# One-column products widened to 128 equal columns, and the odd outputs' row as a full-height product

## The chip, the cores and the metric

The kernel runs on one core of a Trainium2 chip. The metric is device time in microseconds (us) of one execution. The engines are TensorE (PE in the profile, with its weight loads as PEld), VectorE (DVE), ScalarE (ACT), GpSimd (POOL) and SyncE (SP, which here issues DMAs). A float32 matmul is recorded as two MATMUL and two LDWEIGHTS records, so record counts are twice the counts in the code; a float32r matmul is one of each.

## The reference

Attention with decay, an FFT mixer with an FFN behind it, and a gated convolution, on 2 x 768 tokens of 512 features:

```python
x = attention(q, k, v, lam)                       # (2, 768, 512), float32
X = np.fft.fft(np.fft.fft(x, axis=1), axis=2)
u = x + np.real(X)
var = np.mean((u - np.mean(u, -1, keepdims=True)) ** 2, axis=-1, keepdims=True)
un = (u - mean) / np.sqrt(var + 1e-06)
x = u + np.maximum(un @ w_ch1, 0.0) @ w_ch2
out = (sigmoid(causal_conv5(x, conv_w)) * (x @ w_val)) @ w_out
```

The change touches the real part of the FFT and the variance.

## The kernel before

The attention goes by chunks of 128 tokens (6 a batch, `att_*`), the FFT by batch (`fft_*`), the layer norm, FFN and gate by blocks of 384 tokens (k = 0 to 3, two a batch). Features lie on the partitions, in four tiles. There is no loop over the work: `ORDER` is a list of tokens, written out, one for each step (`XD0,1,0` is `fft_D` of batch 0, j 1, w 0; `G0,3,2` is `ffn2`), and each engine runs its part of the list in that order. A plus sign puts an elementwise step on VectorE and not on GpSimd. Weights come as float64 words; the steps `Dl`, `Dx`, `Da`, `Db`, `Dc`, `De` load and convert them to float32 on ACT and DVE between the other work, up to about 200 us. The FFT of batch 0 lies within the attention of batch 1, and the FFT of batch 1 within the FFN of block 0.

The FFT's real part uses symmetry. `fft_pm` (L326) forms sum (w=0) and difference (w=1) of feature pairs, `fft_fold` (L337) adds or subtracts token s and S-s into `F`. `fft_D` (L373) multiplies tiles of `F` (as weights) with the table `cd`: 257 cosine columns for w=0, 256 sine columns for w=1. `fft_P` and `fft_Q` (L399, L389) multiply its result `AB` with the token tables; `fft_P256` (L424) does so for the one column 256. Feature row 0 is special: its even outputs want the sum and its odd outputs the difference. The table has zeros in row 0 at odd columns, and `fft_fx` (L342) forms the row for the odd outputs; `fft_fxh` and `fft_fxl` (L346, L349) split it in two float32r halves, and two one-row matmuls (L376) add it to all odd columns, with a row `oddr` of zeros and ones as the moving operand. In `F` for w=1, row 0 of the first tile meets only sin 0 = 0. `fft_a384` (L357, L359) makes the terms of token 384: eight matmuls whose moving operand is one column, two of them with one row (`odd`), two with one-column weights. `ln_var` (L567) sums squares over the features by a matmul with one column of `ones`, for each 128 tokens: 12 matmuls for block 0 (four tiles each), 3 for each later block. `ln_newton` takes the inverse root on DVE, `ln_diag` (L593, ACT) spreads it on a diagonal and `ln_spread` (L600, TensorE) over the partitions. `pe_fill` (L198) is eight records of `ident` with `ones`, all columns equal, at 8 us. The PSUM pool `ps_o` has two banks; all of these steps take turns in it.

Of the kernel before, what the change touches and what calls it, by code (L numbers as in the profile page):

```python
# [7 lines left out]
F32 = mybir.dt.float32  # L8
F32R = mybir.dt.float32r
AF = mybir.ActivationFunctionType  # L10
# [6 lines left out]
P = 128  # L17
# [26 lines left out]
    "L": "load_chunk", "Z": "pe_fill", "K": "lam_powers", "S": "att_S", "s": "att_pm", "k": "att_kd_act", "A": "att_AV", "E": "att_inter", "T": "att_ST", "t": "att_st", "X": "x_shift",  # L44
    "Xcd": "fft_cd", "Xcs": "fft_cs", "XD": "fft_D", "XA": "fft_a384", "XQ": "fft_Q", "XP": "fft_P", "Xc": "fft_pc",
# [8 lines left out]
    "Kq": "att_qs", "Y": "att_decay", "Xm": "fft_pm", "Xe": "fft_edge", "Xo": "fft_fold", "Xx": "fft_fx", "Xl": "fft_fxl", "Xp": "fft_mp", "Xu": "u_add",  # L54
# [5 lines left out]
Xcs1 S0,0,0 S0,0,1 Z4 L0,1 s0,0,0 s0,0,1 K A0,0 k0,0,0 k0,0,1 L0,2 T0,0 Kq0,1+ e0,0+ k0,1,0 S0,1,0 S0,1,1 t0,0 k0,1,1 T0,1 Y0,1 s0,1,0 L0,3 s0,1,1 A0,1 a0,0 Kq0,2+ t0,1 k0,2,0 S0,2,0  # L60
# [862 lines left out]
```

## Time and profile before

| what | value |
|---|---|
| three runs, us | 455.9, 457.12, 459.17 (median 457.12) |
| the profiled execution's own time, us | 459.33 |
| its span from first to last instruction, us | 457.5 |
| TensorE busy | 447.6 us, 98% |
| VectorE, ScalarE, GpSimd busy | 312.7, 244.6, 129.1 us |
| mean granted TensorE clock | 0.989 |

Busy time says that an instruction was in the engine, not how much it did there; the granted clock is 1.00 at 2.4 GHz and 0.50 at 1.2 GHz. Stages are read by their time from the span's start.

### The profile page before, as it was taken

The numbers are of one execution on the slowest core, as the hardware profiler recorded it, in microseconds if no ns is written. First come the engines' busy times: TensorE is split into PE (matmuls) and PEld (weight loads), VectorE is DVE, ScalarE is ACT, GpSimd is POOL, SyncE is SP. The second block draws the span as 40 slices with busy tenths as digits, with TensorE's granted clock in tenths as the row PEclk, the third lists the DMA queues.
The fourth block names the chain that finished last, engine by engine and source line by source line (L and its number), as shares of the span: only waits on it lengthen the run. The fifth ranks groups of instructions, "written<-read, shape, count | busy, mean of one in ns | idle before, by whom it ended". The sixth has DMA issues, their size and how long they took to land.

```text
span 457.5 us, 7094 instructions
## 1 busy us (share of the span) xinstructions
PE 447.6 (98%) x2752; PEld 396.8 (87%) x2752; DVE 312.7 (68%) x498; ACT 244.6 (53%) x501; POOL 129.1 (28%) x115
## 2 busy tenths in 40 slices
PE   8999999999999999899999999999999999999996
PEld 7887757777658779899999999999999999999994
DVE  5768489887989998885866478813736794222594
ACT  4555566756757765486436357524733844242442
POOL 1132304201041112325263446322523512430230
PEclk9999899889999999999999999999999999999999
DMA  7899951547735340000000000000000010000101
GB/s 266 287 302 318 397 160 65 177 172 255 239 140 185 100 178 1 0 3 0 1 0 24 0 1 23 1 1 24 1 1 0 24 46 1 0 1 24 47 1 69
DMA packets 15861, 40.45 MB, mean 88 GB/s; under 512 B 2012, under 2 KB 4052, under 8 KB 14804
## 3 DMA queue, kind: packets, MB, share of 16 engines
q1 hardware_dynamic: 15540, 39.62, 25.0%
q8 instruction: 21, 0.34, 0.3%
q10 hardware_dynamic: 288, 0.39, 0.3%
q14 instruction: 12, 0.10, 0.1%
HBM read 35.29 MB, written 3.15 MB: 84 GB/s over the span
## 4 chain that ended last, share of the span: by engine, by line
PE 90%; DVE 4%; DMA 2%; SPq 1%; issue 1%; ACT 1%; DVEq 0%; ACTq 0%
PE acc L636 10%; PE acc L638 10%; PE acc L637 10%; PE ph L644 8%; PE ph L638 7%; PE ph L636 7%; PE ph L637 7%; PE pso L636 4%; PE pso L637 4%; PE pso L638 4%; PE pso L373 3%; PE psS L251 3%; PE pso L266 2%; PE pso L277 2%; PE pso L399 2%; PE pso L389 2%
## 5 line engine op out<-in xcount | busy, mean ns | idle before, releaser
L636 PE MATMUL acc<-g,w2s 128*128 128x384 f32 x240 | 83.5, 348 | 1.3 <-DVE tmp L680 1.3
L637 PE MATMUL acc<-g,w2s 128*128 128x384 f32 x240 | 80.5, 335 | 0.0
L638 PE MATMUL acc<-g,w2s 128*128 128x384 f32 x240 | 80.5, 335 | 0.0
L632 POOL TENSOR_TENSOR w2s<-w,w2s 128x512 fp32r<-128x512 f32 x27 | 36.9, 1366 | 145.2 <-ACT w2s L628 130.7
L628 ACT CAST w2s<-w 128x512 fp32r<-128x512 f32 x62 | 37.9, 618 | 42.7 <-PE acc L638 42.7
L665 DVE SCALAR_TENSOR_TENSOR g<-ph,g 128x384 fp32r<-128x384 f32 x60 | 32.8, 553 | 35.3 <-ACT g L660 34.8
L731 DVE SCALAR_TENSOR_TENSOR gate<-u,cw,gate 128x384 f32<-128x384 f32 (+4 forms) x64 | 48.4, 770 | 1.6 <-ACT gate L726 0.9
L636 PEld LDWEIGHTS acc<-g,w2s 128*128 128x128 f32 x240 | 45.1, 188 | 3.7 <-DVE tmp L680 1.6
L614 ACT CAST w1s<-w 128x512 fp32r<-128x512 f32 x48 | 29.6, 618 | 34.5 <-PE ph L638 34.3
L637 PEld LDWEIGHTS acc<-g,w2s 128*128 128x128 f32 x240 | 45.1, 188 | 1.3
L660 ACT ACTIVATE g<-ph 128x384 fp32r<-128x384 f32 x60 | 28.9, 488 | 30.6 <-PE acc L638 17.2
L638 PEld LDWEIGHTS acc<-g,w2s 128*128 128x128 f32 x240 | 45.1, 188 | 0.1
L644 PE MATMUL ph<-uc,w 128*128 128x384 f32 x128 | 45.1, 501 | 0.0
L636 PE MATMUL ph<-hlA,w1s 128*128 128x384 f32 x128 | 43.4, 339 | 0.6 <-DVE g L665 0.6
L638 PE MATMUL ph<-hlA,w1s 128*128 128x384 f32 x128 | 43.1, 337 | 0.2 <-DVE w1s L618 0.2
L637 PE MATMUL ph<-hlA,w1s 128*128 128x384 f32 x128 | 42.9, 335 | 0.0
L618 POOL TENSOR_TENSOR w1s<-w,w1s 128x512 fp32r<-128x512 f32 x21 | 28.2, 1347 | 50.7 <-ACT w1s L614 36.1
L632 DVE TENSOR_TENSOR w2s<-w,w2s 128x512 fp32r<-128x512 f32 x35 | 27.3, 779 | 21.9 <-ACT w2s L628 21.7
L644 PEld LDWEIGHTS ph<-uc,w 128*128 128x128 f32 x128 | 24.8, 197 | 15.0 <-issue 1.4
L618 DVE TENSOR_TENSOR w1s<-w,w1s 128x512 fp32r<-128x512 f32 x27 | 23.0, 859 | 18.6 <-ACT w1s L614 18.6
L636 PEld LDWEIGHTS ph<-hlA,w1s 128*128 128x128 f32 x128 | 24.0, 188 | 1.3 <-DVE g L665 0.9
L638 PEld LDWEIGHTS ph<-hlA,w1s 128*128 128x128 f32 x128 | 24.0, 188 | 0.8 <-DVE w1s L618 0.8
(212 smaller groups left out, 957.4 us busy)
## 6 DMA issues: line engine op xcount, KB each, us to landing
raw<-in_w_dram SPq DMA_DIRECT2D x16, 1024.0 KB, 5.0
ldqk<-in_qT_dram SPq DMA_DIRECT2D x12, 256.0 KB, 5.7
ldqk<-in_k_dram SPq DMA_DIRECT2D x12, 256.0 KB, 5.8
ldv<-in_v_dram SPq DMA_DIRECT2D x12, 256.0 KB, 5.8
ldkT<-in_kT_dram SPq DMA_DIRECT2D x11, 256.0 KB, 6.3
out_dram<-o SPq DMA_DIRECT2D x11, 256.0 KB, 2.0
raw<-in_wv_dram SPq DMA_DIRECT2D x2, 1024.0 KB, 5.0
raw<-in_wo_dram SPq DMA_DIRECT2D x2, 1024.0 KB, 4.7
```

The costliest lines, as they stand in the source:

```text
L251: nc.tensor.matmul(r["pss"][t][:, a, :], r["kT"][hp, a, :], r["qT"][hp, a, :], start=True, stop=True)
L614: self.nc.scalar.copy(w[:, 0], self.raw1(f))
L618: eng.tensor_tensor(w[:, 1], self.raw1(f), w[:, 0].bitcast(F32), op=ALU.subtract)
L628: self.nc.scalar.copy(w[:, 0], self.raw2(f))
L632: eng.tensor_tensor(w[:, 1], self.raw2(f), w[:, 0].bitcast(F32), op=ALU.subtract)
L636: nc.tensor.matmul(out, lh, rh, start=start, stop=False)
L637: nc.tensor.matmul(out, lh, rl, start=False, stop=False)
L638: nc.tensor.matmul(out, ll, rh, start=False, stop=stop)
L644: self.nc.tensor.matmul(ph, self.raw1(f)[:, t], self.uc[k][:, t], start=(t == 0), stop=(t == 3))
L660: self.nc.scalar.activation(g[:, 0], self.ph[(k, f)], AF.Relu)
L665: self.nc.vector.scalar_tensor_tensor(g[:, 1], self.ph[(k, f)], 0.0, g[:, 0].bitcast(F32), op0=ALU.max, op1=ALU.subtract)
L731: self.nc.vector.scalar_tensor_tensor(gp[:, o:TB], x, w, gp[:, o:TB], op0=ALU.mult, op1=ALU.add)
```

## The change

Every product with one moving column now streams 128 columns, all equal. In `fft_a384` the column is repeated by a step of 0, the column groups lie 128 apart in PSUM, the one-row `odd` becomes a tile of 128 rows whose rows 1 to 127 are zero, and the group of one column takes 128 weight columns (of which one output is read). In `ln_var` the whole tile `ones` is the moving operand. `fft_P256` takes 128 weight columns. The row for the odd outputs is written into the spare row 0 of `F` (w=1), and in `fft_D` one float32 matmul of full height adds it to the 128 odd columns (output step 2, moving operand one column of `odd` repeated). `fft_fxh` and `fft_fxl` are gone; `fft_fx` comes after the last fold of its batch, ahead of `fft_D`. `AB` is one column narrower.

```diff
-        self.fx[b] = self.tmp()[0:1]
-        eng.tensor_tensor(self.fx[b], z[0:1, 1, 0, 0:HS], z[:, :, :, S:HS:-1][0:1, 1, 0, :], op=ALU.add)
-    def fft_fxh(self, b):
-        self.fxr[b] = [self.tmp(dt=F32R)[0:1] for _ in range(2)]
-        self.nc.scalar.copy(self.fxr[b][0], self.fx[b])
-    def fft_fxl(self, eng, b):
-        eng.tensor_tensor(self.fxr[b][1], self.fx[b], self.fxr[b][0].bitcast(F32), op=ALU.subtract)
+        eng.tensor_tensor(self.F[b][0:1, 1, 0, :], z[0:1, 1, 0, 0:HS], z[:, :, :, S:HS:-1][0:1, 1, 0, :], op=ALU.add)
...
     def fft_a384(self, b):
-        for g, (c0, cw) in enumerate(((0, 128), (128, 128), (256, 1))):
-            for a in range(2):
-                nc.tensor.matmul(ps[:cw, g:g + 1], cd[:, a, c0:c0 + cw], z[:, 0, a, HS:HS + 1], start=(a == 0), stop=(a == 1 and g > 1))
+        for g in range(3):
+            x = [(cd[:, a, g * P:(g + 1) * P], z[:, 0, a, HS:HS + 1]) for a in range(2)]
             if g < 2:
-                nc.tensor.matmul(ps[:, g:g + 1], self.odd[0:1, 0:128], z[0:1, 1, 0, HS:HS + 1], start=False, stop=True)
+                x.append((self.odd, z[:, 1, 0, HS:HS + 1]))
+            for n, (w, y) in enumerate(x):
+                nc.tensor.matmul(ps[:, g * P:(g + 1) * P], w, y.to_broadcast([P, P]), start=(n == 0), stop=(n == len(x) - 1))
...
     def fft_D(self, b, j, w):
         if w == 0:
-            for x in range(2):
-                nc.tensor.matmul(ps[:, 0:256], self.fxr[b][x][:, sl], self.oddr, start=False, stop=(x == 1))
+            nc.tensor.matmul(ps[:, 1:256:2], F[:, 1, 0, sl], self.odd[:, 1:2].to_broadcast([P, C]), start=False, stop=True, skip_group_check=True)
...
     def fft_P256(self, b):
-            self.nc.tensor.matmul(ps[0:1, 0:HS + 1], self.AB[b][:, j, 256:257], self.cs[0][:, j, :], start=(j == 0), stop=(j == 2))
+            self.nc.tensor.matmul(ps[:, 0:HS + 1], self.AB[b][:, j, 256:384], self.cs[0][:, j, :], start=(j == 0), stop=(j == 2))
...
     def ln_var(self, k):
-                self.nc.tensor.matmul(ps[:, t:t + 1], x[:, t * P:(t + 1) * P], self.ones[:, 0:1], start=(d == 0), stop=(d == len(qs) - 1))
+                self.nc.tensor.matmul(ps[:, t * P:(t + 1) * P], x[:, t * P:(t + 1) * P], self.ones, start=(d == 0), stop=(d == len(qs) - 1))
```

In `ORDER` the tokens move so (batch 0; batch 1 alike):

```diff
-XA0 Xo0,0,0+ Xx0+ Xo0,1,1 Dl0 T1,2 Xo0,0,1+ Xh0 S1,3,0 a1,2 Xl0 S1,3,1 Xo0,1,0+ k1,3,0 XD0,0,0
+XA0 Xo0,0,0+ Xo0,1,1 Dl0 T1,2 Xo0,0,1+ S1,3,0 a1,2 S1,3,1 Xo0,1,0+ Xx0+ k1,3,0 XD0,0,0
```

## Rows read from the trace of the kernel before

**Rows 1.** The page's part 4, the chain that ended last, by engine.

```profile
PE 90%; DVE 4%; DMA 2%; SPq 1%; issue 1%; ACT 1%; DVEq 0%; ACTq 0%
```

**Rows 2.** Span and mean granted clock of the core.

```profile
core 0: 457.5 us, clock 0.989
```

**Rows 3.** Stages: length, busy us (count) of PE, PEld, DVE, ACT, POOL; PEclk; DMA; GB/s.

```profile
41.80:42.60 0.80, 0.00 (x0) 0.00 (x0) 0.80 (x2) 0.00 (x0) 0.77 (x1) 1.00 1.06 387
42.66:44.45 1.79, 1.79 (x16) 1.73 (x16) 1.57 (x3) 0.00 (x0) 0.22 (x1) 1.00 1.10 435
...
45.10:48.40 3.30, 3.30 (x23) 2.89 (x20) 1.02 (x2) 2.39 (x10) 1.66 (x3) 0.50 1.01 395
...
80.25:82.55 2.30, 2.30 (x23) 2.30 (x22) 1.99 (x4) 2.16 (x4) 0.81 (x1) 1.00 0.72 191
82.65:85.95 3.30, 3.30 (x8) 2.09 (x8) 2.82 (x10) 2.91 (x5) 0.56 (x1) 0.50 0.93 332
...
96.35:98.05 1.70, 1.70 (x18) 1.61 (x16) 1.70 (x5) 0.20 (x1) 0.00 (x0) 1.00 1.03 422
...
99.75:103.00 3.25, 3.25 (x8) 2.21 (x7) 1.76 (x2) 1.71 (x4) 0.00 (x0) 0.50 0.29 49
...
187.50:189.70 2.20, 0.93 (x6) 0.61 (x4) 2.20 (x4) 0.62 (x1) 2.20 (x2) 1.00 0.00 0
189.80:193.00 3.20, 3.20 (x19) 3.20 (x20) 3.09 (x4) 1.00 (x2) 1.83 (x2) 1.00 0.00 0
```

**Rows 4.** The chain in order of time, 6 to 13 us: start, us, what.

```profile
6.02 2.08 PE psS L251 x16
8.10 2.00 PE pso L198 x8
...
12.01 1.14 PE psS L251 x16
```

**Rows 5.** The same chain from 40 us on, single steps of TensorE.

```profile
67.02 2.03 PE pso L424 x6
...
80.36 2.75 PE pso L567 x24
...
98.12 1.06 PE pso L373 x4
99.18 0.43 PE pso L376 x2
...
109.87 0.86 PE pso L373 x4
...
123.40 1.94 PE pso L399 x6
```

**Rows 6.** VectorE by stretch and its waits; single lines; timeline rows of ACT, PE, DVE.

```profile
70.90:104.00 33.10, 28.84 (x46) 0.90 0.47 156
104.00:168.60 64.60, 60.47 (x78) 1.00 0.55 187
...
DVE w L489 <- ACT w L485: 3.2, 3, 2.5
...
L342 DVE TENSOR_TENSOR tmp<-pm x2: 548/881/1214, 42.1 to 90.0; 1x384 f32<-1x384 f32 x2
...
L346 ACT CAST tmp<-tmp x2: 494/496/497, 44.8 to 91.4; 1x384 fp32r<-1x384 f32 x2
...
L349 POOL TENSOR_TENSOR tmp<-tmp x1: 984/984/984, 45.4 to 45.4; 1x384 fp32r<-1x384 f32 x1
L349 DVE TENSOR_TENSOR tmp<-tmp x1: 539/539/539, 93.8 to 93.8; 1x384 fp32r<-1x384 f32 x1
...
87.50 0.39 ACT L593 ACTIVATE tmp<-ident,var 128x128 fp32r<-128x128 f32 x1
...
89.42 0.81 PE L600 MATMUL pso<-tmp,onesr 128*128 128x384 f32 x2
...
95.36 1.50 DVE L337 TENSOR_TENSOR F<-pm 128x384 f32<-128x384 f32 x3
```

More of the change, by code (lines that the diff above doesn't have):

```diff
@@ L43 @@
 PLAIN = {
-    "L": "load_chunk", "Z": "pe_fill", "K": "lam_powers", "S": "att_S", "s": "att_pm", "k": "att_kd_act", "A": "att_AV", "E": "att_inter", "T": "att_ST", "t": "att_st", "X": "x_shift",
+    "L": "load_chunk", "Z": "pe_fill", "Kl": "lam_powers", "S": "att_S", "s": "att_pm", "k": "att_kd_act", "A": "att_AV", "E": "att_inter", "T": "att_ST", "t": "att_st", "X": "x_shift",
     "Xcd": "fft_cd", "Xcs": "fft_cs", "XD": "fft_D", "XA": "fft_a384", "XQ": "fft_Q", "XP": "fft_P", "Xc": "fft_pc",
[1 row of a table removed]
[1 row of a table added]
     "Np": "ln_spread",
@@ L53 @@
 GPS = {
-    "Kq": "att_qs", "Y": "att_decay", "Xm": "fft_pm", "Xe": "fft_edge", "Xo": "fft_fold", "Xx": "fft_fx", "Xl": "fft_fxl", "Xp": "fft_mp", "Xu": "u_add",
+    "Kq": "att_qs", "Y": "att_decay", "Xm": "fft_pm", "Xe": "fft_edge", "Xo": "fft_fold", "Xx": "fft_fx", "Xp": "fft_mp", "Xu": "u_add",
     "Ns": "ln_sum", "Nl": "ln_lo", "Na": "ln_acc", "u": "split1l", "v": "split2l", "R": "resid", "Ml": "m_lo", "Mk": "m_gvl",
@@ new lines @@
+F0,10 Nq1,1 v0,11+ Na1,1+ De19 F0,14 Da17 Dl20 Nl1,2+ f0,10 Db17 Nq1,2 h0,10 G0,10,0 Dc15 G0,10,3 Dx17 G0,10,1 De15 G0,10,2 G0,11,0 G0,11,2 f0,14 Dl18 Dc17 G0,11,3 V0,13 G0,11,1 h0,14
+De17 Da20 F0,13 V0,12 Dl16 Db20 Wo0 Nl1,3+ Nq1,3 u1,1+ F1,1 wo0 f0,13 h0,13 Dx18 v0,13+ Dx16 F0,15 Da16 Na1,2+ Db16 Dc16 Na1,3+ U1,0 u1,0+ Wo1 wo1+ Nv1 Dx20 v0,12+ G0,12,0 De16 Dc20
+G0,12,3 Da18 G0,12,1 G0,12,2 Db18 G0,13,3 De20 G0,13,2 f0,15 G0,13,1 V0,14 h0,15 G0,13,0 Wv0 v0,14+ F1,0 V0,15 Dc18 f1,1 Wv2 h1,1 v0,15 G0,14,1 wv2+ U1,3 G0,14,2 G0,15,1 Wv3 G0,14,0
@@ new lines @@
+Rm0,1 G0,15,0 u1,3+ G0,14,3 Rm0,0 G0,15,3 R0,1 R0,0+ F1,2 V1,0 f1,0 v1,0+ Mg0,0 h1,0 G0,15,2 Mg0,1 wv3+ F1,3 f1,2 Rm0,2 h1,2 V1,1 v1,1+ U1,6 R0,2+ Rm0,3 Ha1 G1,0,0 G1,0,3 U1,4 G1,0,1
+u1,6 Mt0,0,3 G1,0,2 G1,1,0 Mt0,0,2 G1,1,2 f1,3 u1,4 h1,3 G1,1,1 V1,2 v1,2+ G1,1,3 F1,4 V1,3 Mt0,0,1 R0,3 v1,3+ G1,2,0 G1,2,1 f1,4 h1,4 G1,2,3 U1,5 u1,5+ F1,6 Mg0,3 Mt0,0,0 Mg0,2 De18
+Ms0,0 F1,5 wv0+ U1,7 Mt0,1,3 Wo2 Mt0,1,2 Wv1 Nw1 u1,7 G1,3,3 G1,2,2 U1,10 G1,3,1 f1,6 G1,3,0 h1,6 V1,4 G1,3,2 Nd1 F1,7 v1,4+ u1,10+ wv1 Mt0,3,3 G1,4,3 f1,5 G1,4,1 U1,8 G1,4,0 V1,5
@@ new lines @@
+U3,13 h3,14 u3,10 Np3 F3,10 u3,13 F3,13 U3,15 u3,15+ G3,8,2 f3,13 Mo2,0 V3,9 h3,13 f3,10 v3,9+ h3,10 G3,9,0 G3,9,1 Me2,0 G3,9,3 G3,9,2 Mo2,1 V3,10 v3,10+ G3,10,0 G3,10,3 G3,10,1 G3,11,0
+G3,11,1 G3,11,3 G3,10,2 G3,11,2 Mo2,2 V3,13 V3,12 v3,13 v3,12+ F3,15 V3,14 V3,15 v3,14+ Me2,2 G3,12,0 v3,15+ f3,15 G3,13,0 G3,14,0 Me2,1 h3,15 G3,15,0 G3,12,1 G3,13,1 Rm3,0 G3,14,1
+R3,0+ G3,15,1 Mz3,0 G3,12,2 Mg3,0 G3,13,2 Rm3,1 Ml3,0 G3,14,2 R3,1+ G3,15,2 Mt3,0,3 Mz3,1 G3,12,3 Rm3,2 Mg3,1 G3,13,3 Ml3,1 G3,14,3 Mt3,1,3 G3,15,3 Mt3,1,2 Ev0,0 Ev1,0 R3,2+ Ev0,1
@@ L109 @@
+Mt3,0,2 Mz3,2 Ev2,0 Mt3,0,1 Mg3,2 Ev3,0 Rm3,3 Ml3,2 Ev1,1 R3,3+ Ev0,2 Ev2,1 Mt3,2,3 Mz3,3 Ev1,2 Mt3,0,0 Mg3,3 Ev2,2 Ml3,3+ Ms3,0 Ev0,3 Mt3,1,1 Ev1,3 Mt3,2,2 Ev2,3 Mx3,0 Ev3,1 Mt3,1,0
+My3,0 Ev3,2 Mt3,2,1 Ms3,1 Ev3,3 Mx3,1 Mk3,0 Eo0,0 Mt3,2,0 My3,1 Eo0,1 Mt3,3,3 Ms3,2 Eo0,2 Mk3,1 Mx3,2 Eo1,0 Mt3,3,2 My3,2 Eo1,2 Mt3,3,1 Eo1,1 Mt3,3,0 Mk3,2+ Eo2,0 Ms3,3 Eo2,2 Mx3,3
+Eo2,1 My3,3 Mk3,3+ Eo3,0 Eo3,2 Es0 Eo3,1 Es2 Es1
 """
@@ L168, in setup @@
         nc.scalar.copy(self.onesr, self.ones)
-        self.odd = self.fft.tile([1, C], F32, name="odd", tag="odd")
+        self.odd = self.fft.tile([P, C], F32, name="odd", tag="odd")
         nc.gpsimd.memset(self.odd, 0.0)
-        nc.gpsimd.memset(self.odd[:, 1:C:2], 1.0)
-        self.oddr = self.fft.tile([1, 2 * C], F32R, name="oddr", tag="oddr")
-        for x in range(2):
-            nc.scalar.copy(self.oddr[:, x * C:(x + 1) * C], self.odd)
+        nc.gpsimd.memset(self.odd[0:1, 1:C:2], 1.0)
         self.U = [p.tile([P, 4, S], F32, name=f"u{b}", tag=f"u{b}") for b in range(B)]
@@ L372, in fft_D @@
         for a in range(2):
-            nc.tensor.matmul(ps[:, 0:n], F[:, w, a, sl], cd[:, a, o:o + n], start=(a == 0), stop=(a == 1 and w == 1))
+            nc.tensor.matmul(ps[:, 0:n], F[:, w, a, sl], cd[:, a, o:o + n], start=(a == 0), stop=(a == 1), skip_group_check=True)
         if w == 0:
-            for x in range(2):
-                nc.tensor.matmul(ps[:, 0:256], self.fxr[b][x][:, sl], self.oddr, start=False, stop=(x == 1))
+            nc.tensor.matmul(ps[:, 1:256:2], F[:, 1, 0, sl], self.odd[:, 1:2].to_broadcast([P, C]), start=False, stop=True, skip_group_check=True)
     def fft_Dev(self, eng, b, j, w):
         if b not in self.AB:
-            self.AB[b] = self.fft.tile([P, 3, 514], F32, name="AB", tag="AB")
+            self.AB[b] = self.fft.tile([P, 3, 513], F32, name="AB", tag="AB")
         n = 257 if w == 0 else 256
-        o = 0 if w == 0 else 258
+        o = 0 if w == 0 else 257
         eng(self.AB[b][:, j, o:o + n], self.psD[(b, j, w)][:, 0:n])
@@ L386, in fft_Q @@
         ps = self.psQ[(b, g)] = self.ps_o.tile([P, 512], F32, name="pso2", tag="pso2")
-        o = 258 + 128 * g
+        o = 257 + 128 * g
         for j in range(3):
@@ L573, in ln_newton @@
         v, sd, r0, a = (var[:, n * j:n * j + n] for j in range(4))
[L574 removed]
+        nc.vector.tensor_scalar_add(v, self.psv[k][:, 0:TB:P], 1e-6)
         nc.scalar.activation(sd, v, AF.Sqrt)
```

85 lines of the change are left out of this document (36 added, 49 removed), and 2 rows, old and new, of the table PLAIN.

## The prediction

> **What bounds the kernel now.** I read the chain that ended last first: nine tenths of it is TensorE, so a microsecond of TensorE is a microsecond of the end, unless another engine fails to follow [rows 1]. Then the mean granted clock: 0.989 over 457.5 us is 5.1 us of full-speed time that TensorE did not get [rows 2]. Where it is lost shows in a table by stage, and the reader is to look at what TensorE did before each fall [rows 3]. It ran at 0.50 (1.2 GHz in place of 2.4) from 45.1 to 48.4, 82.65 to 85.95 and 99.75 to 103.0. Ahead of the first stands an idle stretch of 0.8 us and then, from 42.66 to 44.45, the one-column products of `fft_a384`; ahead of the second, from 80.25 on, the one-column products of `ln_var`; ahead of the third, 96.35 to 98.05, `fft_a384` of the second batch. The page calls TensorE busy in all three, but an instruction there streams one column. Each low stretch, with its edges, is 3.4 us, so it costs 1.7 us; three make 5.1 us, the whole loss. Idleness alone isn't the cause: in 187.5 to 189.7 TensorE worked 0.93 of 2.2 us, and 189.8 to 193.0 is at 1.00 [rows 3].
>
> **The clock.** The change makes these products 128 columns wide. Do 128 equal columns keep the clock where one does not? The nearest rows are at the start: sixteen `att_S` records took 2.08 us at 6.02 and the same sixteen 1.14 us at 12.01, and between them stands `pe_fill`, eight records of 128 columns that are all equal (the profile prints 1.00 there, but the times say the clock doubled in between) [rows 4]. So equal columns go before a rise. I take the three falls as gone: -5.1 us. The first has a rest of doubt, since the idle 0.8 us ahead of it (the wait for the table `cd`) stays.
>
> **The width itself.** `ln_var` of block 0 has 24 records in 2.75 us, 0.115 us each [rows 5]: one column streams in almost no time, so this is what loading the weights takes. 128 columns in float32 are half of 256, and four records of 256 take 0.86 us [rows 5], 0.215 each, so 128 should stream in about 0.108 us, beside the next load of 0.115. The wide form then costs nothing more: the load covers it; with that cover gone it would be 0.11 us for each of 74 records (42 of `ln_var`, 32 of `fft_a384`), 8 us, which is the upper bound. I take 0, since `pe_fill` ran load and stream beside each other: 2.00 us for 8 records [rows 4], 0.25 each at half clock, 0.125 at full. `fft_a384` has 16 records before, 1.79 us in all [rows 3], 0.112 each, and 16 after. Sum 0.
>
> **The odd outputs' row.** Before, one `fft_D` with w=0 is 1.06 us for four records of 257 columns and 0.43 for two one-row records [rows 5], 1.49 in all. After, it has four such records without a switch of shape (4 x 0.217 = 0.87) and two full-height ones of 128 columns (2 x 0.115 = 0.23): 1.10. Six of them save 6 x 0.39 = 2.3 us. What the trace doesn't show is a product whose output steps over every other column, or whose moving operand repeats one column. The bounds are 0.115 a record (nothing lost) and twice 0.115 (each written column takes two slots), which is 6 x 0.23 = 1.4 us; below 0.115 nothing goes, because the weights still load. I take the lower end: the loads of rows 5 bind it either way, and streaming is cheap beside them. The Trainium skill, PSUM — Partial Sum Buffer, section Specifications (TRN2), speaks against the change: "any non-contiguous AP slows matmuls significantly". By that rule the upper end, or more, would hold. No row here shows such a write; the rule has its place among the rivals.
>
> **The column 256.** `fft_P256` takes 2.03 us for six records with one-column weights, `fft_P` 1.94 for six full ones [rows 5]: two batches save 0.2 us.
>
> **What is moved.** `fft_fxh` (ACT, 0.49 us a batch) and `fft_fxl` (POOL 0.98 in batch 0, DVE 0.54 in batch 1) go [rows 6]. `fft_fx` (0.55 us on DVE, 1.21 beside a POOL operation) moves behind the last fold, and now writes a row of F, so the third product of `fft_D` waits for it. In batch 1 the folds end at 96.86 [rows 6]; 0.55 us more is 97.4, and that product starts at 99.18 [rows 5], 1.8 us later. No wait: the gap hides it; without it, 0.55 us. DVE itself gains 0.54 us. Nothing else passes a queue: no DMA is moved, and SP's order stays. A narrower AB, the strided reads of `fft_a384` and `ln_newton` and the larger memset are small operations off the path: 0.
>
> **How much passes on.** TensorE gains 1.7 (first fall) + 3 x 0.39 + 0.1 = 3.0 us by 80 us, 4.7 by 89, and 7.6 by 120. Three things can hold it. First, `ln_spread` starts at 89.42 and needs the last `ln_diag` of ACT, which ends at 87.89 [rows 6]; that work hangs on DVE and moves by 3.0 only, to 84.9, while TensorE arrives at 84.7: 0.3 us of new wait with the signal. Second, VectorE: from 104.0 to 168.6 it is busy 60.47 of 64.6 us, from 70.9 to 104.0 28.84 of 33.1 [rows 6]. It must move by 7 us, and its own idle time is 4.1 and 4.3, plus the 3.0 it gets before 70.9 (where it waits on TensorE), so 11.4 in all. Its longest wait, 2.5 of the 3.2 us in that row, hangs on an ACT that sat behind the third fall [rows 6] and closes with it. So it can follow, not with much over; I put 0.3 us down to it. Third, the stop at 188 (1.27 us) hangs on the accumulators' evictions, which move along: it stays.
>
> Sum against the profiled execution's own 459.33 us (span 457.5 and 1.8 around it): -5.1 - 2.3 - 0.2 + 0.3 + 0.3 = -7.0, so 452.3. That execution is the slowest of the four shown; the median of the three runs is 457.12, and their spread, 455.9 to 459.17, is near two falls of 1.7, which fits runs that had one, two or three of them (it isn't shown). With none after the change, 452.3 stands, and against 457.12 that is -1.05%.
>
> **Rivals.** (a) *VectorE doesn't follow*: its idle time from 104 to 168 is the ACT's and not TensorE's, and doesn't close. Then TensorE keeps only what VectorE had by 104, about 3.0 + 1.0: 455.3. For it: 94% busy there. Against: the releasers of its waits trace to TensorE. (b) *The clock falls anyway*, since it is not the width that counts (only one row of the operand carries data in the new product of `fft_D`): 2.5 us alone, 456.8. Against: `pe_fill`. (c) *The first fall alone stays*, on account of the 0.8 us idle: 454.0. (d) *The stepped write costs double*: 452.3 + 1.4 = 453.7. That is the rule of the PSUM page. (e) *Slower*: a moving operand that repeats one column is read slowly, in the 44 records of `fft_a384` and `fft_D` that have one. All of the 7.6 us is given back at 0.115 + 7.6/44 = 0.29 us a record, and 1% over the median (461.7) is reached at 0.115 + 9.4/44 = 0.33 us; at three times 0.115 it is 462.4. Against it speaks only that the price would have to be that high; no row has such an operand.
>
> **How the numbers follow.** The forecast 452.3 has 0.60, its own range 451.0 to 453.4; (a) 0.12, (b) 0.10, (c) 0.06, (d) 0.08, (e) 0.04. 8 in 10 hold from 450.7 (the 0.6 us of new waits don't come, and the stop at 188 closes) to 456.6, which takes in (a), (c) and (d) and leaves out (e) and most of (b). About 1%, 4.6 us, is what a measurement of this kernel can tell from no change. The line of -1% lies at 452.55, within the forecast's own range: two thirds of the forecast and a little of (d) are below, 0.44. Slower than 461.7 is (e), 0.04; the rest, 0.52, is within 1%.
>
> **What would show it.** Right: no stretch at 0.50 after 42 us and a mean clock near 1.000; 24 records of `ln_var` still in some 2.7 us; one `fft_D` with w=0 in 1.10 us; `fft_P256` at 1.94; VectorE with less idle time between 104 and 168. Wrong: a low stretch behind a wide series; 0.2 us or more for a record of 128 columns; TensorE waiting for DVE around 150 to 170 us, where it hardly waits now.

## The result, and the profile after

Six runs of the changed kernel gave 450.55 to 452.5 us, median 451.04; six runs of the kernel before (the three of the table and three more) 455.9 to 459.17, median 457.85. The medians are 6.8 us apart, 1.5%; the ratio is 0.987, 95% interval 0.984 to 0.991, so it is faster by more than the noise, though by less than 2%. Ratios here and below leave out runs over 1.5% above the fastest of their kernel. The profiled execution took 450.55 us, against the 459.33 of the one before. Its span and mean granted clock, which answer to [rows 2]:

```profile
core 0: 448.8 us, clock 1.000
```

The clock is the first thing to read: no stretch at 0.50 is left before TensorE's work ends. The table by stage, with the columns of [rows 3], shows the places where the falls stood, which now come earlier: behind `fft_a384` (42.6 to 50), under `ln_var` (75.8 to 78.3) and behind it (78.5 to 83.5), behind `fft_a384` of the second batch (92.15 to 96), and last the stop that was at 188:

```profile
42.60:45.00 2.40, 2.40 (x36) 2.13 (x37) 2.05 (x4) 2.37 (x13) 0.41 (x1) 1.00 0.98 399
45.00:50.00 5.00, 5.00 (x40) 4.34 (x39) 2.45 (x8) 2.56 (x4) 1.24 (x2) 1.00 1.04 399
75.80:78.30 2.50, 2.50 (x25) 2.50 (x24) 2.19 (x4) 2.48 (x5) 1.19 (x1) 1.00 0.68 175
78.50:83.50 5.00, 5.00 (x17) 2.95 (x16) 4.46 (x12) 4.43 (x10) 0.08 (x1) 1.00 0.63 220
92.15:96.00 3.85, 3.85 (x21) 3.45 (x20) 3.53 (x4) 3.10 (x9) 0.00 (x0) 1.00 0.03 12
178.70:181.00 2.30, 0.99 (x7) 0.67 (x5) 2.30 (x4) 0.62 (x1) 2.30 (x2) 1.00 0.00 0
```

The chain by engine has hardly moved from [rows 1]: TensorE still sets the end.

```profile
PE 89%; DMA 4%; DVE 4%; SPq 1%; issue 1%; ACT 1%; DVEq 0%; ACTq 0%
```

Its single steps on TensorE answer to [rows 5]. L349 is the widened `fft_a384`, L363 and L365 are the table products and the odd outputs' product of `fft_D`, L413 is `fft_P256` and L388 `fft_P`, L556 is `ln_var`:

```profile
40.57 2.02 PE pso L349 x16
...
44.30 1.06 PE pso L363 x4
45.36 0.22 PE pso L365 x2
45.58 0.87 PE pso L363 x4
46.45 0.22 PE pso L365 x2
...
62.47 1.94 PE pso L413 x6
...
75.72 2.68 PE pso L556 x24
...
90.31 1.79 PE pso L349 x16
92.09 0.87 PE pso L363 x4
92.96 0.22 PE pso L365 x2
...
114.30 1.94 PE pso L388 x6
```

The reader is to see four things: the 24 records of `ln_var` take 2.68 us with 128 columns where they took 2.75 with one; the odd outputs' product is 0.22 us where the one-row pair was 0.43; the table products ahead of it are 0.87 us in one unit and 1.06 in another; `fft_P256` costs what `fft_P` costs.

One caution on the two spans. `fft_a384` starts at 40.57 us here and at 42.66 before [rows 3], and ahead of it only the filling of `odd` was changed: in the profiled executions of this study it starts anywhere between 40.39 and 43.11. So 2.1 of the 8.7 us between the spans are scatter of the start. From the first `fft_a384` to the end it is 414.8 us before (457.5 - 42.66) and 408.2 after (448.8 - 40.57): 6.6 us, against the 7.0 of the prediction's sum.

VectorE did follow, but for 0.3 us. Its row for the same length of work as the second of [rows 6], shifted by the 8.8 us that the work there is early:

```profile
95.20:159.80 64.60, 61.30 (x79) 1.00 0.56 196
```

Its idle time is 3.3 us, from 4.1, and the wait that was longest there, 3.2 us in three with one of 2.5, is now 1.1 in two:

```profile
DVE w L478 <- ACT w L474: 1.1, 2, 0.8
```

At 136.6 us, though, the first product of `ffn1` waits for `relu_lo` (L654), in a row that the kernel before doesn't have there (143 to 149 us):

```profile
PEld ph L633 <- DVE g L654: 0.2, 1, 0.2
```

What the change gave, and where, is read most plainly from the starts of the same step of TensorE in both traces:

| step | before, us | after, us | earlier by, us |
|---|---|---|---|
| first `fft_a384` | 42.66 | 40.57 | 2.09 |
| `fft_P256`, batch 0 | 67.02 | 62.47 | 4.55 |
| `ln_var`, block 0 | 80.36 | 75.72 | 4.64 |
| `ln_spread` | 89.42 | 83.10 | 6.32 |
| first `fft_D`, batch 1 | 98.12 | 92.09 | 6.03 |
| a later `fft_D` | 109.87 | 101.16 | 8.71 |
| `fft_P` | 123.40 | 114.30 | 9.10 |
| `fft_P256`, batch 1 | 135.19 | 126.12 | 9.07 |
| first product behind the last stop | 189.73 | 180.94 | 8.79 |
| end of the span | 457.5 | 448.8 | 8.7 |

### The profile page after: what moved, and what is told of

It reads as the page before. It is cut to its first block, busy times and chain, and to the rows that moved or that the text cites. A ratio compares the mean times of both kernels' runs of the same rounds, so it can differ in the third digit from the quotient of the medians.

```text
span 448.8 us, 7089 instructions
## 1 busy us (share of the span) xinstructions
PE 439.3 (98%) x2752; PEld 393.6 (88%) x2752; DVE 313.0 (70%) x497; ACT 243.7 (54%) x497; POOL 129.2 (29%) x114
## 4 chain that ended last, share of the span: by engine, by line
PE 89%; DMA 4%; DVE 4%; SPq 1%; issue 1%; ACT 1%; DVEq 0%; ACTq 0%
PE acc L627 10%; PE acc L625 10%; PE acc L626 10%; PE ph L633 8%; PE ph L627 8%; PE ph L625 7%; PE ph L626 7%; PE pso L626 4%; PE pso L625 4%; PE pso L627 4%; DMA ldkT<-in_kT_dram 3%; PE pso L363 2%; PE pso L263 2%; PE psS L248 2%; PE pso L388 2%; PE pso L378 2%
## 5 line engine op out<-in xcount | busy, mean ns | idle before, releaser
L654 DVE SCALAR_TENSOR_TENSOR g<-ph,g 128x384 fp32r<-128x384 f32 x60 | 32.8, 553 | 33.3 <-ACT g L649 33.0
L621 DVE TENSOR_TENSOR w2s<-w,w2s 128x512 fp32r<-128x512 f32 x35 | 28.7, 821 | 22.1 <-ACT w2s L617 22.0
L633 PE MATMUL ph<-uc,w 128*128 128x384 f32 x128 | 43.7, 488 | 0.0
L633 PEld LDWEIGHTS ph<-uc,w 128*128 128x128 f32 x128 | 23.8, 190 | 14.7 <-DVE g L654 0.7
L625 PEld LDWEIGHTS ph<-hlA,w1s 128*128 128x128 f32 x128 | 24.0, 188 | 1.3 <-DVE g L654 1.0
L483 ACT ACTIVATE raw<-raw 128x1024 int32<-128x1024 uint32 (+1 forms) x21 | 23.3, 1117 | 2.7 <-DMA raw<-in_w_dram 2.7
```

The source lines that it names most:

```text
L483: self.nc.scalar.activation(w, w.bitcast(U32), AF.Copy, bias=-0.5 + 2.0 ** -17, scale=2.0 ** -29 - 2.0 ** -47)
L621: eng.tensor_tensor(w[:, 1], self.raw2(f), w[:, 0].bitcast(F32), op=ALU.subtract)
L625: nc.tensor.matmul(out, lh, rh, start=start, stop=False)
L633: self.nc.tensor.matmul(ph, self.raw1(f)[:, t], self.uc[k][:, t], start=(t == 0), stop=(t == 3))
L654: self.nc.vector.scalar_tensor_tensor(g[:, 1], self.ph[(k, f)], 0.0, g[:, 0].bitcast(F32), op0=ALU.max, op1=ALU.subtract)
```

## The experiments

The theory: a series of one-column products makes the chip halve the clock of TensorE soon after, and 128 equal columns don't; the rest of the gain is the odd outputs' product without one-row shapes. The rivals: the falls come from the idle time ahead of the series, or from the one-row shapes in it; the width itself costs something; the product with output step 2 or a repeated operand costs something.

Each run lists its mean clock. In the profiled executions one low stretch of 3.3 to 3.4 us takes 0.0037 off it (half of 3.4 over 457), so the mean clock tells how many such lengths an execution lost, also where only its time was taken. Up to 0.002 more goes off at the end, where TensorE has no work left: in the trace of "32 columns" the clock of the last 1.5 us, without one product, is 0.55. So 0.998 counts as none and 0.994 as one. The kernel before varies a good deal. These are 66 of its 79 runs beside the experiments; the other 13 lost five or six lengths and took 460.57 to 464.09 us:

| lost lengths | runs | median us |
|---|---|---|
| none (0.999) | 5 | 453.96 |
| one (0.996) | 24 | 455.26 |
| two (0.992) | 19 | 456.86 |
| three (0.989) | 14 | 458.73 |
| four (0.985) | 4 | 460.17 |

That is 1.55 us a length ((460.17 - 453.96)/4), and it shows why a kernel's median alone says little here: kernels are best compared at an equal number of lost lengths. The counts for all kernels stand in one table behind the experiments.

### First four: parts alone

**ln_var alone.** The kernel before, with `ln_var` as changed:

```diff
-                self.nc.tensor.matmul(ps[:, t:t + 1], x[:, t * P:(t + 1) * P], self.ones[:, 0:1], start=(d == 0), stop=(d == len(qs) - 1))
+                self.nc.tensor.matmul(ps[:, t * P:(t + 1) * P], x[:, t * P:(t + 1) * P], self.ones, start=(d == 0), stop=(d == len(qs) - 1))
```

> The kernel before with ln_var alone made 128 columns wide. My theory: the fall of the clock at 83 us goes and the two behind fft_a384 stay, so 1.7 us less than the kernel before wherever that has this fall: 456.0 to 456.5 against about 457.9, mean clock of the runs up by 0.004, ln_var's 24 records still 2.7 us. Rival, the clock falls for another reason (the idle stretch, the shapes): three falls as before and no change of the time. Rival, width costs: the 24 records take 0.2 us each, 2 us more.

Measured: 456.41 us median (453.91 to 463.08) beside 456.75 for the kernel before, ratio 1.000, interval 0.996 to 1.004. The runs scatter more than any other kernel's: three lost nothing, at 453.91 to 454.28, and that is the kernel before without a fall (453.69 to 454.29 on this chip). So the width of `ln_var` costs nothing, which was expected. The median lies in the expected range by luck only: four runs lost four lengths or more, and against the kernel before it hardly came down. The profile shows the place behind `ln_var` at full clock:

```profile
80.40:83.80 3.40, 3.40 (x12) 1.98 (x11) 2.92 (x10) 3.05 (x6) 0.23 (x1) 1.00 0.93 320
```

The profiled execution is one of the three without a loss: both `fft_a384` had one column there, and no fall came behind them, which was not expected. Where the bad runs lost theirs was not traced. By its time this kernel tells little.

**fft_a384 alone.** The kernel before, with its three groups of columns 128 wide, but the one-row products and the one-column weights kept:

```diff
-                nc.tensor.matmul(ps[:cw, g:g + 1], cd[:, a, c0:c0 + cw], z[:, 0, a, HS:HS + 1], start=(a == 0), stop=(a == 1 and g > 1))
+                nc.tensor.matmul(ps[:cw, g * P:(g + 1) * P], cd[:, a, c0:c0 + cw], z[:, 0, a, HS:HS + 1].to_broadcast([P, P]), start=(a == 0), stop=(a == 1 and g > 1))
...
-                nc.tensor.matmul(ps[:, g:g + 1], self.odd[0:1, 0:128], z[0:1, 1, 0, HS:HS + 1], start=False, stop=True)
+                nc.tensor.matmul(ps[:, g * P:(g + 1) * P], self.odd[0:1, 0:128], z[0:1, 1, 0, HS:HS + 1].to_broadcast([1, P]), start=False, stop=True)
```

> The kernel before with fft_a384 alone 128 columns wide (its one-row and one-column-weight shapes kept). My theory: the falls at 45 and 100 us go, the one behind ln_var stays: up to 3.4 us less where both were there, 454.5 to 456. Rival, the first fall comes of the idle stretch ahead of fft_a384: it stays, 456 to 456.5. Rival, the one-row shapes make the clock fall: all three stay, about 457.9.

Measured: 456.07 us (454.82 to 460.19), ratio 1.002, interval 0.999 to 1.005. In the profile the falls behind both `fft_a384` are gone, and one stretch of double length stays, behind the one-column `ln_var`:

```profile
81.55:88.30 6.75, 6.75 (x14) 4.02 (x15) 6.21 (x13) 4.99 (x11) 0.71 (x1) 0.50 0.55 186
```

The time didn't come down, because the wide series is dear in this form. The chain, L357 with 128 or one weight column and L359 the one-row products:

```profile
42.50 0.68 PE pso L357 x4
43.18 0.41 PE pso L359 x2
43.59 0.64 PE pso L357 x4
44.24 0.41 PE pso L359 x2
44.65 0.53 PE pso L357 x4
```

That is 2.67 us for 16 records, against 1.89 in the chain of the kernel before (42.66 to 44.55, where the next product of the attention begins) and 2.02 in the changed kernel: 0.8 us a batch that only appears where wide products and one-row shapes alternate.

**Both widths.** The two edits above together; only the shapes are still those of before.

> The kernel before with both widened and every one-row shape kept: the clock's part alone. My theory: no fall after 42 us, mean clock 0.999 or more, 452.5 to 453.5, and one fft_D with w=0 still 1.49 us. Rival, the gain came of the shapes: 457 to 458. If the two parts add up, this and the kernel with the shapes alone give the whole gain of 6.8 us.

Measured: 455.63 us (454.44 to 458.17), ratio 0.9995, interval 0.997 to 1.002. Ten of the twelve runs lost nothing, so the falls are gone with the widths alone. Those ten stand at 455.59, 1.6 us above the kernel before without a fall (453.96): twice the 0.8 us of the wide one-row shapes, and 2 us above what was expected. And TensorE still stood idle ahead of the first series in its profile, with no fall behind it:

```profile
PE pso L357 <- DMA cd<-in_cd_dram: 0.7, 1, 0.7
```

**Shapes alone.** The changed kernel, with both series back at one column; every product has full height, and none has one-column weights:

```diff
-                nc.tensor.matmul(ps[:, g * P:(g + 1) * P], w, y.to_broadcast([P, P]), start=(n == 0), stop=(n == len(x) - 1))
+                nc.tensor.matmul(ps[:, g:g + 1], w, y, start=(n == 0), stop=(n == len(x) - 1))
...
-                self.nc.tensor.matmul(ps[:, t * P:(t + 1) * P], x[:, t * P:(t + 1) * P], self.ones, start=(d == 0), stop=(d == len(qs) - 1))
+                self.nc.tensor.matmul(ps[:, t:t + 1], x[:, t * P:(t + 1) * P], self.ones[:, 0:1], start=(d == 0), stop=(d == len(qs) - 1))
```

> The changed kernel with one-column moving operands again in fft_a384 and ln_var (full-height shapes kept): the shapes' part alone. My theory: the falls are back, two or three a run as before, and the time is 2.5 us under the kernel before, 455 to 455.8; one fft_D with w=0 takes 1.09 us. Rival, the one-row shapes made the clock fall: no falls, 451 to 452. Rival, the gain is the clock's alone and the shapes are absorbed by VectorE: 457.5 to 458.

Measured: 454.45 us (452.81 to 456.25), ratio 0.997, interval 0.995 to 1.000. Its stages:

```profile
42.25:44.05 1.80, 1.80 (x18) 1.78 (x20) 1.77 (x3) 0.00 (x0) 1.07 (x2) 0.98 1.02 404
44.05:47.35 3.30, 3.30 (x33) 2.96 (x34) 0.50 (x2) 2.49 (x13) 0.00 (x0) 0.50 1.01 394
78.95:81.50 2.55, 2.55 (x22) 2.44 (x22) 2.25 (x4) 2.53 (x5) 1.43 (x1) 1.00 0.74 191
81.60:84.90 3.30, 3.30 (x7) 1.79 (x6) 2.82 (x10) 2.96 (x6) 0.00 (x0) 0.50 0.92 311
96.50:100.00 3.50, 3.50 (x19) 3.12 (x19) 3.40 (x4) 2.63 (x9) 0.00 (x0) 1.00 0.00 0
```

Without a single one-row shape, the clock falls behind the first `fft_a384` and behind `ln_var`, as before; behind the second `fft_a384` it doesn't. All twelve runs lost at least one length, ten lost two. So the one-row shapes are not what makes it fall. At equal loss this kernel is 2.0 to 2.1 us below the kernel before on the same chip (two lengths: 454.72 against 456.75; one: 453.12 against 455.19): the price of the shapes by themselves.

### The second four: the whole change, and its parts the other way round

**The change again**, unedited, beside the other three.

> The changed kernel once more, many runs beside the kernel before on one chip. My theory: nearly every run has a mean clock of 0.999 or 1.000, and the times lie within 2 us of 451; the runs of the kernel before lie by their number of falls, some 1.6 us each above about 453.9 for none. Rival, the falls come and go for another reason than the one-column products: the changed kernel's runs show one to three falls too, in some of them.

Measured: 451.85 us (451.44 to 455.76, six runs), ratio 0.990, interval 0.986 to 0.994. Five runs lost nothing, one lost one length (the 455.76, which is 3.9 us above the median of the five; only some 1.6 of it is the clock, and the rest wasn't traced).

**Widths without the one-row and one-column shapes.** The kernel before, with `ln_var` as changed and `fft_a384` as changed (full height, 128 columns, a tile `oddf` of its own); the one-row products of `fft_D` and the one-column weights of `fft_P256` stay:

```diff
+        self.oddf = self.fft.tile([P, C], F32, name="oddf", tag="oddf")
...
+                x.append((self.oddf, z[:, 1, 0, HS:HS + 1]))
+            for n, (w, y) in enumerate(x):
+                nc.tensor.matmul(ps[:, g * P:(g + 1) * P], w, y.to_broadcast([P, P]), start=(n == 0), stop=(n == len(x) - 1))
```

> The kernel before with ln_var wide and fft_a384 wide in its full-height form, but the odd outputs' row still by two one-row products, and fft_P256 as before. My theory: no falls; against the changed kernel 6 x 0.39 us for the one-row products, 0.2 for fft_P256 and about 0.45 for a stop of TensorE at 88 us behind fft_fx on VectorE, so 3.0 more: 453.8 to 454.3, and fft_a384 at 1.8 to 2.0 us in place of the 2.67 that it took wide with one-row shapes. Rival, fft_a384 is dear because its operand repeats a column: still 2.67 us and 455.5.

Measured: 453.92 us (452.83 to 456.92), ratio 0.992, interval 0.990 to 0.995; eleven of twelve runs lost nothing. It isolates the clock as far as medians can: 4.2 of the 6.3 us that the changed kernel gains on this chip (458.11 for the kernel before) come with the two widths alone, once the one-row products are out of the wide series. The changed kernel on the same chip is 2.1 us faster still (1.96 between runs that lost nothing, 453.79 against 451.83), which is `fft_D`, `fft_P256` and the moved steps. In the chain, L363 is the wide series, now no dearer than in the changed kernel, and `fft_D` has the old pair of 1.06 and 0.43:

```profile
40.39 1.98 PE pso L363 x16
...
44.08 1.06 PE pso L377 x4
45.15 0.43 PE pso L380 x2
```

**32 columns.** The changed kernel, with 32 equal columns in both series in place of 128:

```diff
-                nc.tensor.matmul(ps[:, g * P:(g + 1) * P], w, y.to_broadcast([P, P]), start=(n == 0), stop=(n == len(x) - 1))
+                nc.tensor.matmul(ps[:, g * P:g * P + 32], w, y.to_broadcast([P, 32]), start=(n == 0), stop=(n == len(x) - 1))
...
-                self.nc.tensor.matmul(ps[:, t * P:(t + 1) * P], x[:, t * P:(t + 1) * P], self.ones, start=(d == 0), stop=(d == len(qs) - 1))
+                self.nc.tensor.matmul(ps[:, t * P:t * P + 32], x[:, t * P:(t + 1) * P], self.ones[:, 0:32], start=(d == 0), stop=(d == len(qs) - 1))
```

> The changed kernel with 32 equal columns in place of 128 in fft_a384 and ln_var, all shapes full height. My theory has no number for where the clock holds: the weights' load sets the time of these products at any of the two widths (24 records of ln_var in 2.7 us either way). If 32 columns are enough, no falls and 451; if the clock wants TensorE streaming most of the time, one or two falls as with one column: 452.7 to 454.5. Rival, only the shapes matter and not the width: no falls.

Measured: 452.8 us (451.56 to 455.6), ratio 0.991, interval 0.988 to 0.995. Two of seven runs lost nothing (451.56 and 451.9, the time of the full change), five lost one or two lengths. In the profile the stretch behind the first `fft_a384` is back:

```profile
43.50:46.85 3.35, 3.35 (x34) 2.91 (x30) 0.58 (x1) 2.34 (x13) 0.00 (x0) 0.50 1.01 401
```

**The odd outputs' product without the step.** The changed kernel, with the same product written to 128 columns that lie side by side:

```diff
-            nc.tensor.matmul(ps[:, 1:256:2], F[:, 1, 0, sl], self.odd[:, 1:2].to_broadcast([P, C]), start=False, stop=True, skip_group_check=True)
+            nc.tensor.matmul(ps[:, 0:128], F[:, 1, 0, sl], self.odd[:, 1:2].to_broadcast([P, C]), start=False, stop=True, skip_group_check=True)
```

> The changed kernel with the third product of fft_D written to columns 0 to 127 side by side in place of the 128 odd ones (the odd outputs' term lands in the wrong columns). My theory: a step of two in the output costs nothing that the weights' load doesn't cover; two records in 0.22 us as in the changed kernel, 451.0 within 0.3. Rival, the rule that a stepped write slows a product: the records get shorter than 0.11 us each, or the product behind them starts earlier, 0.3 to 0.6 us in all six.

Measured: 451.64 us (450.58 to 451.84), ratio 0.987, interval 0.984 to 0.991, beside 451.85 for the changed kernel on that chip. In the chain the product is 0.22 us, as with the step:

```profile
45.56 1.06 PE pso L363 x4
46.62 0.22 PE pso L365 x2
46.85 0.87 PE pso L363 x4
47.72 0.22 PE pso L365 x2
```

The step in the output costs nothing that can be seen here.

### The last three: which series, and 64 columns

**One column in ln_var only**: the changed kernel with the second half of the edit of "Shapes alone".

> The changed kernel with ln_var alone back at one column. My theory: at most one fall a run, behind ln_var at about 82 us, so mean clocks of 0.996 and 1.000 and none of 0.992, and 1.5 us over the changed kernel where it falls: 452.5 to 453.3. Rival, the falls belong to the FFT's shapes: none here, 451 to 451.8.

Measured: 452.45 us (451.27 to 454.48, nine runs), ratio 0.991, interval 0.987 to 0.994. Four runs lost one length, five none; in the profile it lies behind `ln_var` and nowhere else:

```profile
80.40:83.70 3.30, 3.30 (x6) 1.76 (x6) 2.82 (x10) 2.93 (x5) 0.23 (x1) 0.50 0.93 321
```

**One column in fft_a384 only**: the changed kernel with the first half of that edit.

> The changed kernel with fft_a384 alone back at one column (full-height shapes). My theory: at most two falls a run, at about 44 and 96 us, none behind ln_var: mean clocks 0.992 to 1.000, 452.5 to 454.5. Rival, the first fall comes of the idle stretch ahead of fft_a384 and not of the one column: it would have shown in the changed kernel, whose runs beside this one then have 0.996 in some.

Measured: 452.84 us (450.81 to 455.44, twelve runs), ratio 0.993, interval 0.989 to 0.996. Nine runs lost one or two lengths, three none. The profiled execution is one of the three, so that where the others lost theirs is inferred from the edit and not seen.

**64 columns**, by the edit of "32 columns" with 64.

> The changed kernel with 64 equal columns in place of 128 in both series. With 32 the mean clocks went from 0.992 to 1.000, with 128 they are 0.998 to 1.000 in nearly all runs. If 64 are as good as 128: 0.998 to 1.000 and 451 to 452; if as bad as 32: 0.994 in half of the runs and 452.8. The time of the products themselves stays (ln_var 2.7 us).

Measured: 451.78 us (450.61 to 456.42, twelve runs), ratio 0.990, interval 0.987 to 0.994. Eight runs lost nothing, four lost one or two. The profile, one of the four, has a stretch of double length behind the first `fft_a384`:

```profile
44.10:50.85 6.75, 6.75 (x46) 5.92 (x46) 1.50 (x3) 2.48 (x13) 0.62 (x1) 0.50 0.98 346
```

In this execution TensorE stood idle for 1.8 us right ahead of that series, longer than in any other profile, so this one stretch can't be put down to the 64 columns alone:

```profile
PE pso L349 <- DVE F L334: 1.8, 1, 1.8
```

All together, runs by lost lengths (a stretch of double length counts as two; "one-row" says whether one-row products are left in `fft_a384`):

| kernel | columns in fft_a384, ln_var | one-row | none | one | two | three | more |
|---|---|---|---|---|---|---|---|
| before | 1, 1 | yes | 5 | 24 | 19 | 14 | 17 |
| ln_var alone | 1, 128 | yes | 3 | 3 | 2 | 0 | 4 |
| fft_a384 alone | 128, 1 | yes | 5 | 4 | 2 | 1 | 0 |
| both widths | 128, 128 | yes | 10 | 2 | 0 | 0 | 0 |
| shapes alone | 1, 1 | no | 0 | 2 | 10 | 0 | 0 |
| widths, full height | 128, 128 | no | 11 | 1 | 0 | 0 | 0 |
| one column in ln_var | 128, 1 | no | 5 | 4 | 0 | 0 | 0 |
| one column in fft_a384 | 1, 128 | no | 3 | 7 | 2 | 0 | 0 |
| 32 columns | 32, 32 | no | 2 | 4 | 1 | 0 | 0 |
| 64 columns | 64, 64 | no | 8 | 1 | 3 | 0 | 0 |
| the change, twice, and without the step | 128, 128 | no | 17 | 1 | 0 | 0 | 0 |

With 128 columns in both series, 38 of 42 runs lost nothing, whatever the shapes; with one column in both, 5 of 91. Either series alone at one column brings losses back. The width is what counts.

The thirteen traces say the same for `ln_var`, place by place: with one column the clock fell behind it in all four that have it so (before, "fft_a384 alone", "Shapes alone", "One column in ln_var"), with 128 in none of seven, and no idle time lies ahead of it in either. For the first `fft_a384` they say less. With 128 columns it kept the clock in all seven traces, after an idle stretch of up to 1.5 us. With one column it lost it in two (idle 0.9 and 1.0 us ahead) and kept it in two (idle 0.8 us, and none). Behind the second, with one column, only the kernel before fell, and three others didn't.

From the start of the first `fft_a384` to the end, where the scatter of the start drops out, the traces without a loss are close together: 408.2 to 408.3 us for the changed kernel, the change again and the form without the step, 408.1 with one column in `fft_a384`, 410.6 for "widths, full height" and 410.7 for "ln_var alone".

## Why the prediction was right, point by point

**The clock**: right. Three falls were put at 5.1 us. By the starts of the two traces they gave 1.6, 1.7 and 1.7: the second is 6.32 - 4.64; the first is 4.55 - 2.09 less 0.9 (the 1.0 us of `fft_D` below, and 0.13 back for the width); the third is 8.71 - 6.03 less 1.0 for the `fft_D` between, which "ln_var alone", traced without a fall, passes in 10.07 us (94.60 to 104.67) and the changed kernel in 9.07. That is 4.9 in all. The table of the kernel before gives 4.8 (458.73 with three, 453.96 without). What was mis-sized is the comparison with the median: the kernel before loses between none and six lengths in one execution, some two at the median. Of the 6.8 us between the medians, an estimate is 457.85 - 453.96 = 3.9 for the clock, with runs of other chips in the second number, and 2.9 for the shapes with the scatter of the start. The prediction guessed this from the spread of three runs; the 79 runs show it.

**Idleness as the cause** (rival c): wrong for 128 columns. With 0.7 us of idle time ahead of the wide series in "both widths" there is no fall behind it, nor with 1.5 in "One column in ln_var":

```profile
PE pso L349 <- DMA cd<-in_cd_dram: 1.5, 1, 1.5
```

Whether one column in the first `fft_a384` loses the clock without idle time ahead is open: the one such trace kept it. Behind `ln_var` with one column it fell without any.

**The clock falls anyway** (rival b): wrong for 128 equal columns, and partly right for fewer: 32 kept the clock in 2 runs of 7, 64 in 8 of 12.

**The width's own price, 0**: right for `ln_var` (2.68 us against 2.75 [rows 5], and 453.98 at the median of the runs without a fall against 453.96). For `fft_a384` it is 2.02 against 1.89 and 1.79 against 1.66 in the second batch (there to the start of `fft_D`, 98.12 in [rows 5]), 0.13 each. In the second batch the product behind gives that back (0.87 for 1.06), and from the first `fft_a384` to the end 128 columns cost 0.2 us at most (408.2 against 408.1 with one column in full height). And 0 is right only for products of full height: with one-row products between them, the price was 0.8 us a batch. The prediction priced the width as if the two halves of that edit didn't need each other; they do.

**fft_D, -2.3**: right in sign and mechanism, and nearly in size; the place is in part another. Between the traces without a fall of "widths, full height" and the changed kernel, `fft_D` to `fft_P` of the first batch takes 7.79 and 6.77 us (44.01 to 51.80, 44.23 to 51.00), `fft_D` to the FFN of the second 4.70 and 3.91 (93.39 to 98.09, 91.93 to 95.84), and the last unit saves 0.4. That is 2.2 in all. The pair itself gives 0.21 in each of the six units (0.43 to 0.22). The rest is mostly in the product right behind a one-row pair, which takes 1.06 there and 0.87 behind a full-height one, and this isn't always the next unit with w=0. So not every unit went from 1.49 to 1.10: j 0 and j 2 of the first batch, which stand behind a product of the attention, still take 1.06 + 0.22. Which property of the attention's product makes the next four records dearer wasn't tried. By medians "Shapes alone" and "widths, full height" give 2.0 to 2.1 for `fft_D` with `fft_P256` and the moved steps.

**The step in the output and the repeated operand** (rivals d and e): no price. Two records with both take 0.22 us, the same as without the step, which is the lower bound that was taken. The Trainium skill, PSUM — Partial Sum Buffer, section Specifications (TRN2), says that "any non-contiguous AP slows matmuls significantly"; the product with step 2 at 0.22 us, beside 0.22 with the columns side by side, doesn't bear that out for 128 float32 columns behind a weight load. A longer write without that cover was not measured.

**fft_P256, -0.2**: right, 2.03 to 1.94 twice.

**What passes on** (rival a): right, nearly all did. The 0.3 us of new wait ahead of `ln_spread` didn't come. The gains were as forecast, counted from the first `fft_a384`: the last `ln_diag` starts 2.5 us earlier (87.50 [rows 6] to 82.88, less 2.09) where 3.0 was put, TensorE 4.2 where 4.7 was. `ln_diag` ends at 83.27, after the start of `ln_spread`; but `ln_spread` has two products, only its second needs the last `ln_diag`, and the two take 0.81 us together as before. TensorE shows no wait there (timeline rows of the changed kernel: start, us, engine; L582 is `ln_diag`, L589 `ln_spread`):

```profile
82.88 0.39 ACT L582 ACTIVATE tmp<-ident,var 128x128 fp32r<-128x128 f32 x1
...
83.10 0.81 PE L589 MATMUL pso<-tmp,onesr 128*128 128x384 f32 x2
```

The 0.3 us put down to VectorE did come: at 137 us in the changed kernel TensorE loses 0.3 us to `relu_lo` and at 86 us 0.1 to 0.2, and the lead falls from 9.07 to 8.79 us in the table of starts. The stop of 188 us stays: 0.99 us of work in 2.30 at 178.7.

**fft_fx moved, 0**: right where it went, and it bought something that no term had. In "ln_var alone", "both widths" and "widths, full height", where it still runs ahead of VectorE's `relu_lo` and TensorE comes early because no fall held it, TensorE waits for `relu_lo` at 88 us, and VectorE runs the 0.55 us of `fft_fx` right ahead of it (the wait of "ln_var alone", L665 is `relu_lo`):

```profile
PE ph L644 <- DVE g L665: 0.4, 1, 0.4
```

In the changed kernel 0.1 to 0.2 us of it is left. The kernel before shows no such wait: TensorE, late behind the fall, comes after `relu_lo`.

**The sum**: -5.1 (measured -4.9), `fft_D` with the width of `fft_a384` -2.3 (-2.1), `fft_P256` -0.2 (-0.2), waits +0.6 (+0.6: 0.5 on `relu_lo` at 86 and 137 us, the rest in small pieces; half had been put to `ln_spread`). That is -6.6 where -7.0 was forecast, and -6.6 is what the two traces have from `fft_a384` on. That the median, 451.04, still lies below the forecast 452.3 fits the start: the sum began from an execution whose first `fft_a384` came 2.1 us later than in the profiled one after. That part is luck. The lower end of the range is mis-added as well: without the 0.6 us of waits and the stop of 1.27 us it is 450.4 and not 450.7.

**Still open**: why some executions of the kernel before, and of "ln_var alone", lose four lengths or more. Stretches of double length were seen in two kernels and would make such counts, but no profiled execution was one of these. Open too: why the same one-column series keeps the clock in one execution and not in the next.

## What to carry to other kernels

Where the granted clock falls, look at what TensorE streamed before it and not only at whether it was busy: a series of one-column products counts as busy in the profile and still lost the clock, and widening each product to 128 equal columns kept it at next to no cost here (24 records in 2.68 us for 2.75). Do this with products of full height and full width only: one-row and one-column shapes between wide products cost 1.6 us here, as much as one lost length gives back. And where the clock varies between executions, sort the runs by their mean clock before two medians are compared.

## What the runs showed of the hardware that was not expected

- The number of lost lengths varies from run to run of one kernel on one chip, from none to six for the kernel before, at 1.55 us each. A single profile of it is a sample.
- The clock is not kept or lost by a clean limit: 1 of 18 runs of the changed kernel forms lost a length at 128 columns, 4 of 12 at 64, 5 of 7 at 32, 4 of 9 with one column in `ln_var` alone, 9 of 12 with one column in `fft_a384` alone.
- Low stretches come in 3.3 to 3.4 us, or in 6.75 without a break.
- Sixteen records of one column with one-row and one-column-weight shapes take 1.89 us, the same in full height 1.92 with one column and 1.98 to 2.02 with 128, but 128 columns with those shapes 2.67.
